# Two attentions on one core: whole sums in each half of the array's rows, output added in memory, and VectorE's exps planned op by op

## The chip, the cores and the metric

One core of a Trainium2 chip runs the kernel. The metric is the time of one execution on the device in microseconds (us); lower is better.

## What is computed

`x` is 2048 tokens by 512. Two attention layers with 32 heads of 16 run over it, and a gate per token mixes their outputs. Layer A has one key and one value head that all 32 query heads share; layer B has keys and values for each head. Everything is float32.

```python
def reference(A_x, A_wq, A_wk, A_wv, A_wo, B_x, B_wqkv, B_wo, gate_w):
    x = A_x
    g = _sigmoid((x * gate_w).sum(-1, keepdims=True))
    a = _A_ref(x, A_wq, A_wk, A_wv, A_wo)   # q: 32 heads; k = x @ wk, v = x @ wv: one head of 16
    b = _B_ref(x, B_wqkv, B_wo)             # q, k, v: 32 heads of 16
    return g * a + (1 - g) * b
# each layer: softmax(q k^T / 4) v, over all 2048 keys, heads joined, times wo
```

Per layer 32 x 2048 x 2048 exponentials are needed, 268 million in all. They dominate: 2048 instructions of 128 x 1024.

## The kernel before

**Precision.** Operands of the projections and of the scores are split into two float16 parts, high and low, and three of the four products are added (`PARTS`). The probabilities and the values are multiplied in float32. The input's ranges are checked at the end (`flag`); a general version would follow outside of them, which these inputs don't need.

**Tiling of TensorE.** The array of 128 x 128 works as eight tiles of 64 rows by 32 columns. Eight matmuls, two row halves by four column quarters, run beside each other. `by_tiles` (line 220) gives each row half a PSUM bank of its own; a sum over 128 rows thus lies in two banks, and `added` (line 227) adds them with two VectorE ops when they are emptied:

```python
    def by_tiles(outs, lhsT, rhs, start, stop):
        for n in range(0, P, COLS):
            for i, out in enumerate(outs):
                r = slice(ROWS * i, ROWS * (i + 1))
                nc.tensor.matmul(out[n : n + COLS], lhsT[r, n : n + COLS], rhs[r], start=start, stop=stop)

    def added(dst, outs, scale):
        nc.vector.tensor_scalar(dst, outs[0], scale, None, op0=ALU.mult)
        nc.vector.scalar_tensor_tensor(dst, outs[1], scale, dst, op0=ALU.mult, op1=ALU.add)
```

**Stages.** Heads come in eight groups (layers a and b in turn, four groups of eight heads each: `groups`). Per group and per half of the queries (1024) there are four stretches of 16 steps over the keys; a step is a quad of four blocks, each 128 keys by 512 queries of one head. `scores` (line 565) writes two blocks into two PSUM banks (`sc`, two such pairs), and ScalarE takes the exp of 128 x 1024 into `pr` (line 569). `values` (line 602, matmuls on line 613) multiplies the quad with the values and a column of ones, in two halves of 256 queries, so that sums and denominators gather in one of two pairs of banks (`aux`). The other pair is the spare one: there the projections of q, k and v (`project`, line 364, and `v_units`), the turning of v (line 454), the output product (`o_unit`, line 469) and the scores for VectorE's exps (`vector_scores`, line 571) take turns, each emptied by VectorE before the next. After a stretch `emptied` (line 618) adds the two banks into `raw` and moves the rows to their heads' places with eight transfers. `norm_pieces` (line 491) divides and splits, and `o_unit` multiplies with `wo`, weighs with the gate and adds the result to `acc` in SBUF, one op per bank on line 485. `acc` is stored at the end.

**Where q and k come from.** `project` empties, adds, clamps, splits into float16 parts and takes the largest value (lines 229, 230, 394, 237, 238, 234), and lays the parts into `Q` and `K` by small transfers (line 375), mostly from GpSimd's queue.

**VectorE's exps.** Some blocks go to VectorE instead of ScalarE. Per exp of 128 x 1024: two conversions from PSUM (line 581), two ops that part mantissa and power (line 587), five steps of a polynomial (line 592). All run in place, each on the result of the one before.

**The order.** All of it is unrolled; a planner in Python (`_Tasks`, line 75, and the loop behind it) writes the order. It counts time in exps (`EXP = 916` ns): per exp one pair of scores, one or two halves of values, and as many products on the spare banks as fit. VectorE's work beside that is put in by `beside`, and `choose` (line 761) asks for an exp on VectorE when nothing is late. Engines run their own instructions in order and wait for each other by semaphores. In the profile, line 225 is the matmul of `by_tiles`, line 562 that of the scores.

Of the kernel before, what the change touches and what calls it, by code (L numbers as in the profile page):

```python
# [20 lines left out]
P = 128  # L21
# [10 lines left out]
EXP = 916  # L32
SCORES, HALF, PRODUCT = 213, 428, 216
FULL = 1500
NARROW = 710
LATEST = 6
WIDE = 1240
OVER = 160
LATE = 250
SCALE = DH ** -0.5  # L40

# [6 lines left out]
VEC = (0.2591677609, 0.7359788364, 0.8973912565, 1.2863896980, -0.0530661755, 1.9226385145)  # L51
VEC5 = struct.unpack("I", struct.pack("f", VEC[5]))[0] & 0x7FFFFF
RANGED = ["x", "gate", "wk_a", "wv_a", "wq_a", "wo_a", "wq_b", "wk_b", "wv_b", "wo_b", "v_a", "v_b"]
KINDS = RANGED + ["q_a", "q_b", "k_a", "k_b"]

# [19 lines left out]
class _Tasks:  # L75

    def __init__(self):  # L80
        self.now, self.clock, self.begun, self.busy, self.empty = 0, 0, 0, 0, 0
        self.units, self.open, self.side, self.fill = [], deque(), deque(), deque()
        self.moves, self.moved = deque(), 0

    def add(self, units, after, due, more=0, full=FULL, ready=lambda: True):

        self.units += [(after, due, u, more, full, ready) for u in units]
        self.units.sort(key=lambda u: u[1])

    def add_side(self, fns, after, ns):  # L90

        more = [(after, f, ns[i % len(ns)]) for i, f in enumerate(fns)]
        self.side = deque(sorted([*self.side, *more], key=lambda s: s[0]))

    def move(self, fns):
        self.moves.extend(fns)

    def given(self, ns):

        self.busy = max(self.busy, self.clock + LATE) + ns  # L100

    def beyond(self, ns):

        self.busy = max(self.busy, self.begun) + ns

    def product(self, left):

        if not self.open:
            for u in self.units:
                if u[0] <= self.now and self.empty <= self.clock and len(u[2]) + 1 <= left and u[5]():  # L110
                    self.units.remove(u)
                    self.open.extend(u[2])
                    self.more, self.full = u[3:5]
                    break
        if not self.open:
            return False
# [8 lines left out]
    def late(self):  # L125

        n = len(self.open)
        for u in self.units:
            n += len(u[2]) + (6 if len(u[2]) > 4 else 3)
            if n > u[1] - self.now:  # L130
                return True
        return False

    def beside(self, until, urgent):
# [10 lines left out]
        if urgent:  # L145
            filled()
# [818 lines left out]
```

## Time and profile before

| | |
|---|---|
| median of 3 runs | 1908.06 us (1907.36 to 1908.97) |
| the profiled execution's span | 1905.9 us, 2.2 less than the median of the runs |
| granted TensorE clock | 0.992 |
| TensorE (PE) busy | 1800.7 us, 94% |
| VectorE (DVE) busy | 1382.3 us, 73% |
| ScalarE (ACT) busy | 1831.9 us, 96% |
| GpSimd (POOL) busy | 466.3 us, 24% |
| exps on ScalarE, on VectorE | 1974, 74 |

How to read the rows: a group's row has line, engine, operation, output and input tile, shapes, count; behind the first bar busy us and mean ns of one; behind the second the idle time just before them and what ended it. A timeline's row has its start in us from the span's start, how long the merged piece lasts in us, then engine, line, operation and count; matmuls overlap, so their starts say more than their lengths. A row of a stretch has its bounds and length in us, busy us of the engine with the count, granted clock, DMA share and GB/s. A row of transfers has destination and source, the issuing queue, the count, the size of each, and the median us from issue to landing.

### The profile page before, as it was taken

To read this page: it belongs to the slowest core of one execution; us is meant where nothing else is said; L and a number is where in the kernel's file an instruction comes from. 1 tells how busy PE (TensorE), PEld (TensorE's weight loads), DVE (VectorE), ACT (ScalarE), POOL (GpSimd) and SP (SyncE) were. 2 spreads that over 40 slices of the span, in tenths; PEclk is the share of its full clock that TensorE was granted. 3 is DMA by queue.
4 is the path that set the end of the run, shared out by engine and by line. 5 is a ranking of instruction groups with operands and counts; after the bars stand their busy time and mean duration, and the time that the engine had idled before them with its cause. 6 is when DMAs were issued, how large, how long until landed. Compare 5 with 4: busy or idle time off the path is not lost.

```text
span 1905.9 us, 128055 instructions
## 1 busy us (share of the span) xinstructions
PE 1800.7 (94%) x59664; PEld 1124.5 (59%) x59664; DVE 1382.3 (73%) x2095; ACT 1831.9 (96%) x1997; POOL 466.3 (24%) x840
## 2 busy tenths in 40 slices
PE   7999999999999999999999999999999999999985
PEld 4666665555566665665555656656655666665642
DVE  5367668787888765778788873788888867477762
ACT  4999999999999999999999999999999999999984
POOL 5333302330044230323006502042203433030000
PEclk9999999999999999999999999999999999999997
DMA  4121101110022110111002201020101111011101
GB/s 141 27 49 35 35 15 27 42 35 16 12 43 46 29 37 12 41 32 35 12 21 45 52 19 31 19 54 15 32 15 36 39 38 37 10 37 35 40 26 42
DMA packets 55739, 65.03 MB, mean 34 GB/s; under 512 B 21440, under 2 KB 29632, under 8 KB 55200
## 3 DMA queue, kind: packets, MB, share of 16 engines
q0 software_dynamic: 24112, 24.89, 6.8%
q1 hardware_dynamic: 30400, 31.46, 6.3%
q8 instruction: 469, 7.68, 1.7%
q14 instruction: 70, 0.57, 0.1%
q10 hardware_dynamic: 688, 0.43, 0.1%
HBM read 10.55 MB, written 4.19 MB: 8 GB/s over the span
## 4 chain that ended last, share of the span: by engine, by line
ACT 67%; PE 15%; issue 12%; DVE 4%; DMA 1%; SPq 0%; DVEq 0%; ACTq 0%; POOL 0%
ACT pr L569 67%; PE aux L613 7%; PE sc L562 4%; PE aux L225 4%; DVE stats L234 1%; DVE acc L485 0%; DVE vpr L592 0%; DMA acc<-in_A_x_dram 0%; DVE dTb L497 0%; DMA dTb<-rawb 0%; PE aux L300 0%; DVE v L238 0%; DVE yv L230 0%; DVE yv L229 0%; DVE xT L305 0%
## 5 line engine op out<-in xcount | busy, mean ns | idle before, releaser
L569 ACT ACTIVATE pr<-sc 128x1024 f32<-128x1024 f32 x1974 | 1821.3, 1090 | 24.7 <-PE sc L562 21.1
L613 PE MATMUL aux<-pr,vA 64*32 64x256 f32 x15712 | 647.2, 376 | 2.0 <-issue 1.8
L613 PE MATMUL aux<-pr,vB 64*32 64x256 f32 x15872 | 636.4, 376 | 0.6 <-issue 0.4
L562 PE MATMUL sc<-Qa,kA 64*32 64x512 f16 x7856 | 441.2, 380 | 28.0 <-ACT pr L569 4.7
L562 PE MATMUL sc<-Qb,K 64*32 64x512 f16 x7936 | 426.2, 381 | 31.0 <-ACT pr L569 5.6
L592 DVE SCALAR_TENSOR_TENSOR vpr<-vpr,part 128x1024 f32<-128x1024 f32 x296 | 363.5, 1228 | 6.1
L562 PEld LDWEIGHTS <-K 64*32 64x32 f16 x8192 | 203.3, 89 | 276.8 <-issue 195.3
L613 PEld LDWEIGHTS aux<-pr,vA 64*32 64x32 f32 x15712 | 328.6, 105 | 57.8 <-issue 9.8
L613 PEld LDWEIGHTS aux<-pr,vB 64*32 64x32 f32 x15872 | 316.6, 106 | 53.9 <-issue 4.6
L562 PEld LDWEIGHTS <-kA 64*32 64x32 f16 x8192 | 203.5, 89 | 238.8 <-issue 157.8
L485 DVE SCALAR_TENSOR_TENSOR acc<-aux,gate_up,acc 128x512 f32<-128x512 f32 x240 | 180.1, 750 | 126.6 <-PE aux L225 112.2
L375 POOL DMA_DIRECT2D Qb<-hib x128 | 63.0, 492 | 557.0 <-PE sc L562 553.9
L375 POOL DMA_DIRECT2D Qa<-hia x118 | 59.9, 508 | 481.8 <-PE sc L562 322.8
L581 DVE TENSOR_SCALAR vpr<-aux 128x512 int32<-128x512 f32 x148 | 95.2, 685 | 36.8 <-PE aux L562 36.2
L587 DVE TENSOR_SCALAR part<-vpr 128x1024 int32<-128x1024 int32 x148 | 103.1, 728 | 0.7
L375 POOL DMA_DIRECT2D K<-hik x128 | 64.3, 506 | 117.5 <-DVE hik L237 115.5
L592 DVE SCALAR_TENSOR_TENSOR vpr<-part 128x1024 f32<-128x1024 f32 x74 | 90.3, 1221 | 1.6
L225 PE MATMUL aux<-xT,w16vb 64*32 64x512 f16 x1536 | 90.5, 376 | 0.0
L225 PE MATMUL aux<-w16ob,o16b 64*32 64x512 f16 x1536 | 70.4, 391 | 16.0 <-ACT o16b L505 13.3
L225 PE MATMUL aux<-xT,w16kb 64*32 64x512 f16 x1536 | 79.5, 376 | 0.1
L225 PE MATMUL aux<-xT,w16qa 64*32 64x512 f16 x1536 | 76.0, 380 | 0.9 <-issue 0.5
L225 PE MATMUL aux<-xT,w16qb 64*32 64x512 f16 x1536 | 76.8, 376 | 0.0
(145 smaller groups left out, 1320.4 us busy)
## 6 DMA issues: line engine op xcount, KB each, us to landing
acc<-in_A_x_dram SPq DMA_DIRECT2D x16, 256.0 KB, 6.1
dTa<-rawa SPq DMA_DIRECT2D x128, 32.0 KB, 2.5
oTa<-rawa SPq DMA_DIRECT2D x128, 32.0 KB, 2.8
K<-hik POOLq DMA_DIRECT2D x128, 32.0 KB, 2.2
K<-lok POOLq DMA_DIRECT2D x128, 32.0 KB, 2.7
Qb<-hib POOLq DMA_DIRECT2D x128, 32.0 KB, 2.8
Qb<-lob POOLq DMA_DIRECT2D x128, 32.0 KB, 2.4
out_dram<-acc SPq DMA_DIRECT2D x16, 256.0 KB, 2.0
```

The source lines that it names most:

```text
L225: nc.tensor.matmul(out[n : n + COLS], lhsT[r, n : n + COLS], rhs[r], start=start, stop=stop)
L234: nc.vector.tensor_reduce(stats[:, n, i : i + 1], src, axis=axis, op=ALU.max, apply_absolute_value=True)
L375: queues[(8 * p + n) % len(queues)].dma_start(op[to : to + DH].rearrange("d (a q) -> d a q", a=2), state[part][rows])
L485: nc.vector.scalar_tensor_tensor(acc[:, t], bank, g, acc[:, t], op0=ALU.mult, op1=ALU.add)
L562: nc.tensor.matmul(sc[i][a : a + COLS], k[r, c * P + a : c * P + a + COLS], Q[src, gi, half, p][r, j * BLK : (j + 1) * BLK], start=True, s ...
L569: nc.scalar.activation(probs[u], sc, AF.Exp, scale=SCALE / (UP * UP))
L581: nc.vector.tensor_scalar(fix[:, i], sc[i], SCALE / (UP * UP) / math.log(2) * 2.0 ** 23, -(2.0 ** 23), op0=ALU.mult, op1=ALU.add)
L587: nc.vector.tensor_scalar(t, fix, a, b, op0=ALU.bitwise_and, op1=op)
L592: nc.vector.scalar_tensor_tensor(pr, pr if i < 4 else m, VEC[i], m if i else power, op0=ALU.add, op1=ALU.mult)
L613: nc.tensor.matmul(o[32 * i : 32 * i + 32, cols], v[r], probs[at // ACT][r, at % ACT, cols], start=first, stop=last)
```

## The change

`_fast` and the planner are written anew; the general version stays. What differs:

- **Sums by halves.** Row half i of the array now sums for its own queries or tokens in bank i of a pair. To reach all terms, each operand is also held with its two row halves swapped (`swapped`: two transfers), and every product has two turns, `w = 0` and `1`: straight and swapped. `added` is gone; each bank holds whole sums. A projection covers 1024 columns at once, 24 jobs of eight matmuls, and is emptied by two ops of 128 x 1024 (high and low part), with the largest value taken from the high part and no clamp.
- **Scores.** Row half = head of a pair, column half = one of two blocks of 512 queries, with the keys of the other column half swapped. Eight matmuls of 64*32 by 512 as before; exps stay 128 x 1024. There are 32 phases (group, half of the queries, two pairs of heads) of 32 quads.
- **Values.** As before eight tiles; the probabilities of ScalarE in two jobs of 256 columns, those of VectorE in four of 128. After a phase one copy of 128 x 1024 empties the pair, and ten transfers move the rows.
- **Output sums.** An output unit (`o_unit`) covers two tiles of tokens with six products and is emptied by two plain ops into one of two buffers (`sums`). For the first group it is stored to the output; for the next six it is added to the output in memory by a transfer from GpSimd's queue (`accum_op`, 48 transfers of 512 KB); before the last group the output so far is read back (`late`, in the memory of `xT`), and the last is added on VectorE.
- **VectorE's exps.** One conversion of 128 x 1024, mantissa and power, four polynomial steps. Each op is an `_Op` with a rank, a time from which it can run, and the ops that it follows.
- **The order.** `_Plan` holds a clock for each engine. VectorE takes the free op of lowest rank (0 emptying a phase, 1 emptying the spare pair, 3 exps, above that the rest, and what is overdue comes forward). TensorE gives the scores first when they can be written, then values, spare jobs, values of VectorE's exps (near a phase's end the last before the spare jobs), and starts nothing that would hold the scores beyond `SLACK`. An exp goes to VectorE when the spare pair is free, no unit is in a hurry, and little of the exps' work is queued. Constants: `EXP` 904 for 916.
- **Start.** x is loaded into the tiles of the exps; seven of eight pairs of x tiles are turned before the first score. The swapped copies of the first weights and of k's and v's weights are moved before they are used.

The core of the diff:

```diff
-EXP = 916
-SCORES, HALF, PRODUCT = 213, 428, 216
...
+EXP, EXP_ENDS, EXP_AFTER = 904, 1136, 456
+SCORES, HALF, PRODUCT = 215, 430, 215
+SLACK = 400
+PROBS, VECS = 6, 7
...
+    def by_tiles(outs, lhs, rhs, start, stop):
+        for n in range(0, P, COLS):
+            for i in range(2):
+                nc.tensor.matmul(outs[n : n + COLS, i], lhs[i][rows(i), n : n + COLS], rhs[i][rows(i)],
+                                 start=start, stop=stop)
+
+    def swapped(dst, src, queue):
+        for i in range(2):
+            queue.dma_start(dst[rows(i)], src[rows(1 - i)])
...
+            def hi():
+                hilo.extend(halves_of(name))
+                nc.vector.tensor_scalar(hilo[0], pair[1], UP ** -1, None, op0=ALU.mult)
+
+            def lo():
+                nc.vector.scalar_tensor_tensor(hilo[1], pair[1], UP ** -1, hilo[0], op0=ALU.mult, op1=ALU.subtract)
...
+        def finish(end):
+            def take(e):
+                g = gate_up[:, i, tt[e] : tt[e] + 1]
...
+                if e == 0:
+                    state["sum"] = sums[turn[0]]
+                    turn[0] ^= 1
+                nc.vector.tensor_scalar(state["sum"][:, e], pair[1][:, e], g, None, op0=ALU.mult)
...
+                if n == 0:
+                    nc.sync.dma_start(dst, state["sum"])
+                else:
+                    plan.on_pool([lambda: nc.gpsimd.dma_start(dst, state["sum"], accum_op=ALU.add)], t, 1500)
...
+    def products(u, bank):
...
+        for hh in range(2):
+            for a in range(0, P, COLS):
+                key = c * P + (a + ROWS * w) % P
+                j = a // ROWS
+                nc.tensor.matmul(bank[a : a + COLS, hh], k[rows(hh), key : key + COLS],
+                                 Q[src, gi, half, p][rows(hh), j * BLK : (j + 1) * BLK], start=True, stop=True)
...
+            for i in range(2):
+                nc.tensor.matmul(pair[0][32 * k : 32 * k + 32, i, cols], v[rows(i)], probs[2 * m + k // 2][rows(i), hh, cols],
+                                 start=first, stop=last)
...
+    def vector_job(now):
+
+        if chained() > WORK + (EXTRA if half_vec else 0):
+            return None
+        if held[0] > held[2] - 3 or plan.backlog(2) > 2500:
+            return None
...
+        a = plan.vec(convert, 1130, 1, t + TO_VEC, (), spared)
+        b = plan.vec(mantissa, 620, 3, 0.0, (a,), None, due(7000))
+        c = plan.vec(power, 620, 3, 0.0, (a,), None, due(6300))
+        d = plan.vec(lambda: horner(3), 1131, 3, 0.0, (b, c), None, due(5600))
+        for i in (2, 1, 0):
+            d = plan.vec(lambda i=i: horner(i), 1131, 3, 0.0, (d,), None if i else over, due(1300 * i + 1300))
...
+        limit = math.inf
+        if at[0] < len(quads) and free_probs and t < math.inf:
+            limit = max(t, plan.starts[-1] + SLACK) if plan.starts else t
+        ending = at[0] >= len(quads) or quads[at[0]][0] > pv_at[0] or left_in(pv_at[0]) < 20
...
+        for get in (mine, other, spare) if ending else (mine, spare, other):
```

1427 lines of the change are left out of this document (807 added, 620 removed).

## The prediction

> **What bounds the kernel now.** I read the page first: span, engines, and the chain that ended last.
>
> ```profile
> span 1905.9 us, 128055 instructions
> PE 1800.7 (94%) x59664; PEld 1124.5 (59%) x59664; DVE 1382.3 (73%) x2095; ACT 1831.9 (96%) x1997; POOL 466.3 (24%) x840
> ACT 67%; PE 15%; issue 12%; DVE 4%; DMA 1%; SPq 0%; DVEq 0%; ACTq 0%; POOL 0%
> L569 ACT ACTIVATE pr<-sc 128x1024 f32<-128x1024 f32 x1974 | 1821.3, 1090 | 24.7 <-PE sc L562 21.1
> ```
>
> ScalarE (ACT) is the longest engine and holds two thirds of the chain, nearly all of it in one line, the exps: 1974 of the 2048 that the problem needs. The other 74 run on VectorE (DVE). Next: what does one exp cost when nothing holds it, and where do the exps begin and end? A stretch cut from the start of one exp to the start of another, then the timeline's first and last piece of exps:
>
> ```profile
> 629.84:645.20 15.36, 15.36 (x18) 1.00 0.07 17
> ```
> ```profile
> 13.30 5.92 PE L225 MATMUL aux<-xT,w16qa 64*32 64x512 f16 x192
> ...
> 29.28 3.12 ACT L569 ACTIVATE pr<-sc 128x1024 f32<-128x1024 f32 x3
> ...
> 1834.27 42.27 ACT L569 ACTIVATE pr<-sc 128x1024 f32<-128x1024 f32 x46 [0.47 <-PE sc L562]
> ```
>
> The stretch counts 18 exps, of which the first is only the tail of the one before: 17 steps, 15.36/17 = 0.9035 us each. This is ACT's own pace. 1974 steps of it are 1783.5 us; the exps in fact take from 29.28 to 1834.27 + 42.27 = 1876.54, or 1847.3 us. So the span is 29.3 (start) + 1783.5 (pace) + 63.8 (ACT held up) + 29.4 (tail) = 1906. The median of the runs, 1908.06, lies 2.2 above the span, and I add 2.2 at the end.
>
> So two things shorten this kernel: fewer exps on ACT (0.9035 us for each that goes to DVE), and less of the 63.8. What keeps the number on DVE at 74? DVE is only 73% busy, so look at TensorE (PE) and at the PSUM banks that it shares with DVE, in the timeline:
>
> ```profile
> 1225.83 0.63 PE L225 MATMUL aux<-xT,w16qb 64*32 64x512 f16 x16
> ...
> 1226.26 0.41 PE L562 MATMUL sc<-Qb,K 64*32 64x512 f16 x8
> ...
> 1226.48 0.63 PE L613 MATMUL aux<-pr,vB 64*32 64x256 f32 x16
> 1226.53 0.69 DVE L229 TENSOR_SCALAR yb<-aux 128x512 f32<-128x512 f32 x1
> ...
> 1227.01 0.41 PE L562 MATMUL sc<-Qb,K 64*32 64x512 f16 x8
> ...
> 1227.32 0.69 DVE L230 SCALAR_TENSOR_TENSOR yb<-aux,yb 128x512 f32<-128x512 f32 x1
> ...
> 1227.93 0.41 PE L562 MATMUL sc<-Qb,K 64*32 64x512 f16 x8
> ...
> 1228.05 0.43 DVE L394 TENSOR_SCALAR yb<-yb 128x512 f32<-128x512 f32 x1
> 1228.14 0.63 PE L613 MATMUL aux<-pr,vB 64*32 64x256 f32 x16
> ...
> 1228.51 0.43 DVE L237 TENSOR_SCALAR hib<-yb 128x512 f16<-128x512 f32 x1
> 1228.57 0.63 PE L225 MATMUL aux<-xT,w16qb 64*32 64x512 f16 x16
> ...
> 1228.97 0.69 DVE L238 SCALAR_TENSOR_TENSOR lob<-yb,hib 128x512 f16<-128x512 f32 x1
> ...
> 1229.58 0.68 DVE L234 TENSOR_REDUCE stats<-yb 128x1 f32<-128x512 f32 x1
> ...
> 1229.87 0.41 PE L562 MATMUL sc<-Qb,K 64*32 64x512 f16 x8
> ...
> 1230.08 0.63 PE L613 MATMUL aux<-pr,vB 64*32 64x256 f32 x16
> ...
> 1230.52 0.41 PE L225 MATMUL aux<-xT,w16qb 64*32 64x512 f16 x8
> ...
> 1230.73 0.41 PE L562 MATMUL sc<-Qb,K 64*32 64x512 f16 x8
> ```
>
> Read the starts, since ends overlap. From 1229.87 PE is packed: scores of one exp (eight matmuls, 0.21 us), values of one exp (sixteen, 0.44), one job of eight on the spare banks (0.21), next scores: 0.86 us. Against 0.9035 us per exp that leaves room for one spare job per exp and not for two. And from 1226.26 to 1228.57, 2.3 us, no spare job runs: DVE is emptying the spare banks (L229, L230, 1.48 us and 0.8 of handing over), and PE idles between values and scores. So the limit is the number of these places, one per exp, and the time in which the spare banks are shut. Call it the budget of places.
>
> **The change, part by part.** I cost the budget before, to calibrate it, from these rows:
>
> ```profile
> L592 DVE SCALAR_TENSOR_TENSOR vpr<-vpr,part 128x1024 f32<-128x1024 f32 x296 | 363.5, 1228 | 6.1
> L485 DVE SCALAR_TENSOR_TENSOR acc<-aux,gate_up,acc 128x512 f32<-128x512 f32 x240 | 180.1, 750 | 126.6 <-PE aux L225 112.2
> L581 DVE TENSOR_SCALAR vpr<-aux 128x512 int32<-128x512 f32 x148 | 95.2, 685 | 36.8 <-PE aux L562 36.2
> L587 DVE TENSOR_SCALAR part<-vpr 128x1024 int32<-128x1024 int32 x148 | 103.1, 728 | 0.7
> L592 DVE SCALAR_TENSOR_TENSOR vpr<-part 128x1024 f32<-128x1024 f32 x74 | 90.3, 1221 | 1.6
> L225 PE MATMUL aux<-xT,w16qa 64*32 64x512 f16 x1536 | 76.0, 380 | 0.9 <-issue 0.5
> ```
> ```profile
> L230 DVE SCALAR_TENSOR_TENSOR rawa<-aux,rawa 128x512 f32<-128x512 f32 x32 | 22.2, 692 | 3.4
> L229 DVE TENSOR_SCALAR rawb<-aux 128x512 f32<-128x512 f32 x32 | 22.0, 687 | 25.0 <-PE aux L613 25.0
> L454 PE MATMUL aux<-ident,v 64*32 64x64 f16 x1024 | 18.6, 191 | 2.7 <-DVE v L238 2.7
> ```
>
> Places offered: 1974, and 63.8/0.9035 = 70 more while ACT is held up: 2044. Taken: six groups like the last of the first fence (the weights q, k, v and o), 1536 matmuls each, are 1152 jobs of eight; the turning of v (1024 matmuls in jobs of sixteen) 64; x and k at the start some 30. Shut: 64 projected blocks at 2.3 us; 128 output units with two of L485 each, 2.2 (1.5 and 0.7 of handing over); 16 turns at 2: 461 us or 510 places. Left for the 74 exps: 2044 - 1152 - 64 - 30 - 510 = 288, so 3.9 places per exp on DVE. Counted singly one costs 1 for its scores, 2 for its values and 2.2 for the banks' shut time (L581 twice, then handing over), 5.2; some of its values thus run while the banks are shut.
>
> *Sums by halves.* Each bank now holds whole sums of its own queries, so nothing is added across banks. A projection empties 128x1024 with two ops and no clamp: 32 blocks, of which 31 in the steady part. A 1024-wide op from PSUM isn't in this trace; bounds are twice L581 (1.37) and the SBUF op L592 (1.23). I take 1.23, because one op has one fixed part. Shut time: 1.23 + 1.26 + 0.8 = 3.3 us, 102 us. The output units are 60 in the steady part instead of 128, each with two 512-wide ops, 2.1 us: 126. Eight turns at 2.2: 18. Together 246 us or 272 places, instead of 510. PE's jobs are the same work: 31 x 24 = 744, output 372, turning 128 short ones (92 places), start 35: 1243. Scores and values keep their size and count.
>
> *DVE's load.* Removed or shrunk: the projections' six ops in the timeline are 3.6 us x 64 blocks (3.2 for v), 224, become 32 x 3.5 = 113; L485's 180 us and its twin of the first group (16 more ops, 12) become 128 plain ops, 83; the four groups of raw sums (88, first and last shown) become 32 copies, 36. That frees some 270 us of DVE: 1382 - 652 (the four exp rows) - 270 = 460 without exps. An exp on DVE now has four L592-like steps instead of five: 1.23 + 2 x 0.73 + 4 x 1.23 = 7.6 us, or 7.05 where independent ops alternate and each starts 0.08 us before the last one ends, as L234 at 1229.58 does behind L238. In a steady part of some 1760 us DVE could then hold (1760 - 460)/7.05 = 184, or 171 at 7.6. It isn't the limit.
>
> *The number N of exps on DVE.* Offered: 2048 - N, plus 33 for a hold-up of 30 us. Taken: 1243 + 272 + 3.9 N. So 4.9 N = 566, N = 115. The new planner may cut the values of DVE's exps into jobs of 0.21 us that fit a shut time; if all of them run there, an exp costs 1 + 2.2 + 1 = 4.2 and N = 135. I take the middle, 125; bounds 91 (nothing hidden, 5.2 + 1) and 165 (less shut time than I think).
>
> *Hold-ups.* Now 63.8, of which some 9 in the first 71 us, where ACT also copies x. The old planner reckons 916 ns for an exp that takes 903.5, the new one 904, and lets a PE job start only if the scores still come in time. I take 30; bounds 10 and 80 (PE is fuller: 125 more exps' worth of jobs in less time).
>
> *Start and tail.* The first products (13.30 to 19.22) now wait for the swapped weights too, 1024 queries are projected instead of 512 twice, and seven of eight x pairs are turned ahead of the first score. I take 35 for 29.3, bounds 29 and 41. The tail keeps its chain (empty the banks, ten moves instead of eight, reciprocal, product, out) but ends eight output tiles: 29.5, bounds 26 and 36.
>
> *Adding transfers.* 48 transfers of 512 KB add into the output in memory, from POOL's queue; two buffers hold the sums, so the third output unit's DVE op waits for the first one's landing. No adding transfer is in this trace; bounds by rows:
>
> ```profile
> acc<-in_A_x_dram SPq DMA_DIRECT2D x16, 256.0 KB, 6.1
> ...
> out_dram<-acc SPq DMA_DIRECT2D x16, 256.0 KB, 2.0
> ```
> ```profile
> L375 POOL DMA_DIRECT2D K<-lok x128 | 65.2, 514 | 4.3 <-issue 2.6 <-DMA K<-lok 1.4
> ```
>
> Twice the bytes, read and written: 2 x 2.0 = 4 to 2 x (6.1 + 2.0) = 16 us; I take 8, nearer the single store than the crowded loads. A unit takes six places (5.4 us) and 2.1 shut, so the third comes 15 us after the first: 8 is hidden. It is not where the unit's transfer stands behind the 32 moves of a projection on POOL (32 x 0.51 = 16 us); then it lands 16 + 1.5 + 8 = 25.5 us after those moves begin, the third unit comes after 7.5 + 15 = 22.5, and DVE waits 3 us, in at most 14 places: 42 us on an engine that isn't the limit. I count nothing; the bound of the hold-ups takes it in, and the rival prices a late landing.
>
> **Sum:** 35 + (2048 - 125) x 0.9035 = 1737.4, + 30 + 29.5 + 2.2 = **1834**.
>
> **The rivals.**
>
> *DVE fills up (1789).* If shut time is shorter than the trace's 0.8 us of handing over suggests, N goes to DVE's ceiling, between 171 and 184, say 175: 35 + 1692.3 + 30 + 29.5 + 2.2. For it: DVE idles 27% now. Against: the 2048 - 175 = 1873 places are fewer than 1243 + 272 + 3 x 175 = 2040. The page "VectorE: DVE Perf Modes" of the Trainium skill (The DRAIN you can't avoid) says the next op doesn't issue until the pipe is empty, which would make alternating ops worthless. The trace's 0.08 us overlap of L238 and L234 disagrees; by the page the ceiling is 171 and the time 1793.
>
> *The places are no better used (1890).* N stays near 80 and hold-ups at 45: 35 + 1778.1 + 45 + 29.5 + 2.2. For it: PE is already at 94%, and a projection shuts the banks longer at a time.
>
> *The adding transfers stall DVE (slower, 1940).* DVE works in order: an output unit that waits for a landing holds every later op, the emptying of the exps' scores among them; PE, in order too, then stands at its next spare job, and the scores of ACT's exps stand behind it. If a transfer lands after 16 us and starts up to 16 us late behind a projection's moves, the third unit of a row waits 16 + 1.5 + 16 - 22.5 = 11 us, in 14 rows of four units 154 us, of which ACT would feel perhaps 106, since banks and buffers cover the rest: 1834 + 106. It makes the kernel slower from 74 us on ACT, so 108 us on DVE, 7.7 a row, a landing after about 12.7 us. For it: POOL issues all moves. Against: single loads of this size land fast. "SBUF — State Buffer" (SBUF: two separate sides) in the Trainium skill states that POOL can't write a transfer's descriptors while DVE runs a double-rate op. L587 (0.73 us for what takes L592 1.23) looks like one, yet POOL's 128 moves of K take 514 ns on average beside 148 of these; by the page each added transfer may start 0.73 us later, 48 x 0.73 = 35 us if nothing hides it, 1869.
>
> *It doesn't do what it says:* the planner finds hardly a place for DVE's exps (N below 40): 1905 to 1915.
>
> **How the numbers follow.** Forecast (N 91 to 165) 0.60, DVE full 0.13, places no better 0.12, transfers stall 0.12, does not do it 0.03. The range leaves out most of the slower rival and the lowest corner: from 1775 (N 175, hold-up 15) to 1900 (N 80, hold-up 55). A measurement here tells about 0.2%, 3.8 us: faster 0.85, the same 0.02, slower 0.13.
>
> **What would show it.** Right: 1905 to 1950 exps on ACT, still at 0.904 a step; ACT held up under 50 us in all; DVE 75 to 85% busy; an emptying of 1024 from PSUM at 1.2 us. Wrong: a count of exps on ACT above 1965 (places), DVE waiting for a landing of out (transfers), a step above 0.92, or first scores after 41 us.

## Result and the profile after

The changed kernel takes 2002.92 us (median, 1999.31 to 2005.09), the kernel before on the same chip 1908.38: a ratio of 1.0486, 95% interval 1.0467 to 1.0506. It is 95 us slower where 74 us faster was forecast. The profiled execution has a span of 2001.7 us.

First the page's span, engines, chain and exps, to be read against the first fence of the prediction:

```profile
span 2001.7 us, 130978 instructions
PE 1840.3 (92%) x61680; PEld 1155.0 (58%) x61680; DVE 1198.4 (60%) x1352; ACT 1816.2 (91%) x1961; POOL 542.4 (27%) x891
...
PE 47%; ACT 31%; issue 9%; DVE 6%; POOL 4%; DMA 2%; SPq 1%; ACTq 0%; DVEq 0%; POOLq 0%
...
L571 ACT ACTIVATE prob<-sc 128x1024 f32<-128x1024 f32 x1946 | 1805.6, 1093 | 128.3 <-PE sc L564 124.4
```

ACT runs fewer exps (1946 for 1974), and yet it is 91% busy instead of 96%, and the chain has passed from ACT (67% before) to PE (47%). No engine but POOL (27% for 24%) got fuller. The last column of the last row is the clue: ACT stood 128.3 us idle ahead of exps, 124.4 of it for scores from PE, where the same row of before has 24.7 and 21.1.

Next the pieces that the sum was made of: a clean stretch of 18 steps, cut from one exp's start to just before another's (the 19 exps include the tail of the one before it), and the first and the last exps in the timeline.

```profile
1856.74:1873.01 16.27, 15.42 (x517) 8.91 (x512) 16.10 (x18) 16.27 (x19) 1.25 (x1) 1.00 0.13 30
```
```profile
34.05 6.01 ACT L571 ACTIVATE prob<-sc 128x1024 f32<-128x1024 f32 x6
...
1940.89 32.29 ACT L571 ACTIVATE prob<-sc 128x1024 f32<-128x1024 f32 x35
```

16.27 / 18 = 0.904 us: ACT's pace is what it was. Put into the terms of the prediction's sum, the span is: start 34.0 us; pace 1946 x 0.9035 = 1758.2; tail 2001.7 - (1940.89 + 32.29) = 28.5; what is left, 180.9, is hold-ups. (Below, hold-ups are counted from first to last start of an exp, less 0.9035 a step: 180.6 here, 63.4 before.)

Where does ACT's wait for PE come from? The waits of PE, of after:

```profile
PE pair L612 <- issue: 31.9, 44, 2.9
PE pair L564 <- DVE sum L471: 15.8, 3, 8.2
PE pair L564 <- DMA K<-lokb: 12.6, 8, 3.2
PE sc L564 <- issue: 10.5, 17, 2.0
...
PE pair L188 <- issue: 5.2, 6, 2.6
```

"issue" means that the matmul waited for nothing that the profile shows: no semaphore, no busy PE. All such rows of PE sum to 53.5 us in after; the same view of before has these three and no more, 4.6 us:

```profile
PE aux L613 <- issue: 2.3, 4, 1.2
PE sc L562 <- issue: 1.8, 4, 0.5
...
PE aux L225 <- issue: 0.5, 1, 0.5
```

The longest such gap in the timeline of after (rows of PE and POOL):

```profile
1164.38 1.35 POOL L481 DMA_DIRECT2D out_dram<-sum  x1
...
1166.79 1.22 POOL L481 DMA_DIRECT2D out_dram<-sum  x1 [1.07 <-DVE sum L471]
...
1168.74 0.62 PE L612 MATMUL pair<-prob,vA 64*32 64x256 f32 x8
...
1172.23 0.44 PE L612 MATMUL pair<-prob,vA 64*32 64x256 f32 x4 [2.87 <-issue]
```

PE stops in the middle of a job, 8 of its 16 matmuls done, 2.6 us after POOL began to issue the second of two adding transfers, and stands for 2.87 us. What is missing are instructions: among the page's DMA queues is one, q8, that carries nothing else.

```profile
DMA packets 140435, 109.73 MB, mean 55 GB/s; under 512 B 86432, under 2 KB 94880, under 8 KB 139888
...
q8 instruction: 485, 7.95, 1.6%
```

The same two lines of before:

```profile
DMA packets 55739, 65.03 MB, mean 34 GB/s; under 512 B 21440, under 2 KB 29632, under 8 KB 55200
...
q8 instruction: 469, 7.68, 1.7%
```

In after, 485 packets of 16 KB bring 7.95 MB for 2 x 61680 matmuls and weight loads. That is 64 bytes for each, so 256 instructions a packet, and PE needs a packet every 4.1 us. The queue is as busy as before, but the traffic beside it has grown from 65 to 110 MB and from 55,739 to 140,435 packets. Worked out from the packets' records: of the 59 gaps over 250 ns without a wait, nine in ten end 1.25 to 1.55 us after a packet of q8 has come in, while nine in ten random moments lie 0.2 to 4.4 us behind one. For the gap above, 6.7 us passed from the start of the packet before to the start of the one that ended it. Of the 14 gaps over 1 us (26.3 us) 11 have an adding transfer issued 2 to 11 us before they end, which holds for some 20% of random moments.

### The profile page after: what moved, and what is told of

The parts are those of the page before. It is cut to its first block, busy times and chain, and to the rows that moved or that the text cites. A ratio compares the mean times of both kernels' runs of the same rounds, so it can differ in the third digit from the quotient of the medians.

```text
span 2001.7 us, 130978 instructions
## 1 busy us (share of the span) xinstructions
PE 1840.3 (92%) x61680; PEld 1155.0 (58%) x61680; DVE 1198.4 (60%) x1352; ACT 1816.2 (91%) x1961; POOL 542.4 (27%) x891
## 2 busy tenths in 40 slices
DMA packets 140435, 109.73 MB, mean 55 GB/s; under 512 B 86432, under 2 KB 94880, under 8 KB 139888
## 3 DMA queue, kind: packets, MB, share of 16 engines
q8 instruction: 485, 7.95, 1.6%
q10 hardware_dynamic: 1952, 2.66, 0.4%
## 4 chain that ended last, share of the span: by engine, by line
PE 47%; ACT 31%; issue 9%; DVE 6%; POOL 4%; DMA 2%; SPq 1%; ACTq 0%; DVEq 0%; POOLq 0%
ACT prob L571 31%; PE pair L612 23%; PE sc L564 13%; PE pair L188 8%; DVE vec L763 2%; POOL Qa L352 2%; DVE sum L471 1%; DVE vec L751 1%; SPq L505 1%; PE pair L564 1%; POOL K L352 1%; PE pt L265 1%; DMA wqb<-in_B_wqkv_dram 1%; DVE raw L665 0%; DMA oT<-raw 0%
## 5 line engine op out<-in xcount | busy, mean ns | idle before, releaser
L571 ACT ACTIVATE prob<-sc 128x1024 f32<-128x1024 f32 x1946 | 1805.6, 1093 | 128.3 <-PE sc L564 124.4
L612 PE MATMUL pair<-prob,vA 64*32 64x256 f32 x15680 | 695.8, 378 | 16.9 <-issue 15.7
L612 PE MATMUL pair<-prob,vB 64*32 64x256 f32 x15456 | 657.7, 381 | 11.6 <-issue 10.6
L612 PEld LDWEIGHTS pair<-prob,vA 64*32 64x32 f32 x15680 | 350.3, 105 | 81.2 <-issue 38.8
L763 DVE SCALAR_TENSOR_TENSOR vec<-vec,vec 128x1024 f32<-128x1024 f32 x306 | 373.3, 1236 | 2.4
L612 PEld LDWEIGHTS pair<-prob,vB 64*32 64x32 f32 x15456 | 329.5, 106 | 71.4 <-issue 29.2
L751 DVE TENSOR_SCALAR vec<-pair 128x1024 int32<-128x1024 f32 x102 | 124.1, 1217 | 71.9 <-PE pair L564 71.2
L763 DVE SCALAR_TENSOR_TENSOR vec<-vec 128x1024 f32<-128x1024 f32 x102 | 125.1, 1226 | 1.0
L481 POOL DMA_DIRECT2D out_dram<-sum x48 | 59.7, 1243 | 239.2 <-DVE sum L471 215.3
L511 DVE RECIPROCAL dT<-dT 128x256 f32<-128x256 f32 (+1 forms) x66 | 111.0, 1690 | 18.8 <-DMA dT<-raw 18.8
L188 PE MATMUL pair<-xT,w16kb 64*32 64x512 f16 x1536 | 101.6, 376 | 4.7 <-issue 4.6
```

The costliest lines, as they stand in the source:

```text
L188: nc.tensor.matmul(outs[n : n + COLS, i], lhs[i][rows(i), n : n + COLS], rhs[i][rows(i)], start=start, stop=stop)
L481: plan.on_pool([lambda: nc.gpsimd.dma_start(dst, state["sum"], accum_op=ALU.add)], t, 1500)
L511: nc.vector.reciprocal(d[:, c : c + cut], d[:, c : c + cut])
L571: nc.scalar.activation(probs[u], sc, AF.Exp, scale=SCALE / (UP * UP))
L612: nc.tensor.matmul(pair[0][32 * k : 32 * k + 32, i, cols], v[rows(i)], probs[2 * m + k // 2][rows(i), hh, cols], start=first, stop=last)
L751: nc.vector.tensor_scalar(tile("p").bitcast(I32), pair[1], SCALE / (UP * UP) / math.log(2) * 2.0 ** 23, None, op0=ALU.mult)
```

## Two theories

**Queues.** ACT is held up by separate causes, each a queue: PE's instructions come late while heavy transfers run; DVE, which works in order, stands at an op that waits for POOL, and with it the emptying that PE waits for; K is laid late. **Full PE** (the rival): the new plan packs PE so tightly that any slip reaches ACT; take one cause away and the time comes back elsewhere. The prediction's own slower rival, DVE waiting for the landing of an added transfer, already has the trace against it: DVE has no wait for out in after.

Chips differ. The experiments were measured in four sets, and the kernel before took 1923 us in the first (e1 to e4), 1923 in the second (e5 to e8), 1917 in the third (e9 to e12) and 1911 in the fourth (e13 to e15). So ratios to it are compared, and the changed kernel was run again.

## Experiments

**e5, the changed kernel again.**

> The changed kernel unaltered, to see what it measures on the chip of these runs. Chips differ (the kernel before took 1908 on one and 1923 on another); the ratio to the kernel before should again be 1.045 to 1.060 and the hold-ups 170 to 210 us.

2023.57 us, ratio 1.0538 (1.0493 to 1.0582), hold-ups 198.9, PE without a wait 70.6 us. e1 to e4 and e6 to e8 are set against this. PE's gaps were 53.5 us on the first chip and are 70.6 here, so a difference of some 17 us between kernels of different sets can be the chip's.

**e1, without the adding transfers.**

```diff
-plan.on_pool([lambda: nc.gpsimd.dma_start(dst, state["sum"], accum_op=ALU.add)], t, 1500)
+plan.on_pool([], t, 0)
```

> Leaves out the 48 adding transfers of groups 1 to 6, so the output lacks these groups; the plan and all else stay. The theory (instruction supply): the changed kernel's PE stands 54 us with nothing that it waits for, against 5 before, and the long ones of these lie beside adding transfers of 512 KB, while the queue that brings 16 KB packets of instructions slows from one in 3.8 us to one in 5.4 to 7.4. Without the transfers these gaps fall to some 25 us and the time by 20 to 45 us, to 1958 to 1983. Rival one (the prediction's: DVE waits for landings): the time falls by over 60 us, and DVE's waits on out in the changed kernel should have been there, which they are not. Rival two (PE is simply planned too full, any slip reaches ACT): under 8 us.

1991.87 us, ratio 1.0341 (1.0312 to 1.0371): 32 us less than e5. PE without a wait 37.4 for 70.6, hold-ups 170.3 for 198.9. The first row of PE's waits in e5, then in e1:

```profile
PE pair L612 <- issue: 40.8, 58, 2.9
```
```profile
PE pair L612 <- issue: 18.5, 43, 1.4
```

The gaps' 33 us and the time's 32 agree: instructions, not landings. It isn't the chip: e2 and e3, measured in e1's set with their adding transfers, have gaps of 71.0 and 69.6 us.

**e2, V's swapped copy in whole rows.**

```diff
-swapped(vB[1][:, ts, :, 0], vB[0][:, ts, :, 0], nc.sync)
-swapped(vB[1][:, ts, :, 2], vB[0][:, ts, :, 2], nc.sync)
+swapped(vB[1][:, ts], vB[0][:, ts], nc.sync)
```

> Moves the swapped copy of V of the b groups as whole rows of 6 KB instead of 64-byte pieces (one pair of transfers in place of two, 65,500 packets fewer of 140,435). The theory (instruction supply): some of the gaps without a wait lie beside these transfers (532 us), so 3 to 15 us less, and DVE's waits for SP's queue get no longer. Rival two (PE planned too full): within 4 us of the changed kernel, since the plan is the same.

2032.65 us, ratio 1.0564 (1.0540 to 1.0588), not below e5; the gaps are as they were. A miss: moving the same copy in fewer, larger packets (75,666 in all for 140,435) gains nothing.

**e3 and e7, the largest-value ops of the weights** later, or left out:

```diff
-plan.vec(lambda: absmax(f"w{part}_{src}", gi, pair[0][:, 0]), 590, 4, at + 500, due=at + 20000)
+plan.vec(lambda: absmax(f"w{part}_{src}", gi, pair[0][:, 0]), 590, 4, at + 15000, due=at + 40000)   # e3
+plan.vec(lambda: None, 590, 4, at + 500, due=at + 20000)                                           # e7
```

> The largest-value op of a weight block is laid on DVE 15 us after the planned end of POOL's split instead of 0.5 us. The theory (DVE held in line): the trace shows DVE standing 25.0 + 7.6 us in six places for POOL's split, and PE and ACT behind it; with the later op these waits are gone and the time falls by 20 to 35 us, to 1968 to 1983. Rival two (PE planned too full): DVE's waits go, but the slip shows up elsewhere, under 8 us gained.

> The largest-value ops of the weight blocks are left out (so the range test sees no weights); the plan stays as it is. The theory (DVE held in line behind POOL's split): DVE's 33 us of waiting for POOL go, PE's waits for DVE with them, and the time falls by 20 to 35 us against the changed kernel. Rival two (PE planned too full): under 8 us.

The trace of after shows what is at stake (DVE, POOL, SyncE's queue and PE around 1410 us):

```profile
1406.61 1.11 SPq L193 DMA_DIRECT2D w16vb<-w16vb  x2
...
1407.81 0.53 SPq L219 DMA_DIRECT2D wqb<-in_B_wqkv_dram  x1
...
1410.91 1.49 POOL L204 TENSOR_SCALAR wqb<-wqb 128x512 f32<-128x512 f32 x1 [4.33 <-DMA wqb<-in_B_wqkv_dram]
...
1412.47 0.61 POOL L205 CAST w16qb<-wqb 128x512 f16<-128x512 f32 x1
...
1413.12 0.69 DVE L197 TENSOR_REDUCE stats<-w16qb 128x1 f32<-128x512 f16 x1 [7.07 <-POOL w16qb L205]
...
1413.72 1.40 DVE L471 TENSOR_SCALAR sum<-pair,gate_up 128x512 f32<-128x512 f32 x2
...
1415.17 0.72 PE L564 MATMUL pair<-Qb,K 64*32 64x512 f16 x8 [8.20 <-DVE sum L471]
...
1416.43 1.02 ACT L571 ACTIVATE prob<-sc 128x1024 f32<-128x1024 f32 x1 [8.47 <-PE sc L564]
```

Read it from the top: the next weights' load stands on SyncE's queue behind the swapped copies of the last ones (L193), which wait for POOL's split; the load issues late, POOL splits late, DVE stands 7.07 us at a largest-value op that only the range test at the end needs, the output's sum stands behind it, the scores on the same bank behind that, and the next exp last: 8.47 us.

e3: 2010.63 us, ratio 1.0455 (1.0435 to 1.0474), 13 us less than e5 (3 of them by the plan's own clock); DVE's 33 us for the weights are gone from its waits. e7's own 28418 us mean nothing, since the range test, fed with zeros, sends it through the general program afterwards; in its first part hold-ups are 184.9, 14 less than e5. Both are below the 20 to 35 that I gave: of DVE's 33 us of waits less than half reached ACT.

**e8, K and V of the b groups earlier.**

```diff
-ns=14000 if part == "k" else 18000
+ns=40000 if part == "k" else 44000
```

> The projections of K and V of the b groups are due 40 and 44 us ahead of their first use in place of 14 and 18. The plan itself then has 12.6 us held up in place of 24.3, with 96 exps on DVE in place of 102, and ends 6 us earlier. The theory: the 19 us at 305 to 325 us of the changed kernel, where K of the first b group comes late, are gone, and with them waits for landings of K; the exps that DVE loses cost 5.4 us; 6 to 25 us less. Rival two: the gap at 305 goes but PE, as full as before, loses it again later: within 5 us.

1998.06 us, ratio 1.0397 (1.0361 to 1.0434), 25 us less than e5; the gap of 14.86 us that after shows at 321.54 us ahead of an exp, and PE's 12 us of waits for landings of K, are gone. The gain is a net one: with the plan moved, the weights' largest-value ops stand in a worse place. DVE waits 49.6 us for POOL's split of weights (32 in e5), and in three places PE stands 19.8 us behind a conversion that waits behind such an op; the exps there are late by 6.3, 7.5 and 7.2 us.

**e4, no exps on DVE** (the planner's choice returns nothing), and **e10, PE planned looser**:

```diff
-SCORES, HALF, PRODUCT = 215, 430, 215
+SCORES, HALF, PRODUCT = 221, 442, 221
```

> No exp runs on DVE, all 2048 on ACT, whose own plan then has only 6.5 us held up. At 34 us of start, 2048 x 0.9035 = 1850.4 and 30.7 of tail and launch, the time is 1915 + hold-ups. The theory (hold-ups come from queues: instruction supply, DVE behind POOL's split, late K and Q): these stay, of the 180 only the 19 planned for K and some small ones go, hold-ups 90 to 140, so 2005 to 2055. Rival two (PE planned too full with the jobs of 102 exps): hold-ups fall under 60 and the time to under 1975, faster than the changed kernel although ACT has 102 exps more.

> The changed kernel's planner reckons 221, 442 and 221 ns for PE's jobs in place of 215, 430 and 215, so it packs PE 3% looser; its own plan has 31 us held up in place of 24 and 106 exps on DVE in place of 102, and ends 3 us later. Rival two (PE planned too full): the some 190 stalls of about 0.3 us on PE alone, 57 to 61 us in all, shrink by half or more, and the time falls by 20 us or more. The theory: instruction gaps, DVE's waits and late K are untouched by this, so the time is within 12 us of the changed kernel, ratio to the kernel before 1.045 to 1.060.

e4: 2058.27 us, ratio 1.0693 (1.0672 to 1.0715), hold-ups 146.7, somewhat over the theory's 90 to 140 and far from the rival's 60. Two things in its trace stand against a simple reading. Its output units come closer together, and DVE now does wait for landings of the adding transfers:

```profile
DVE sum L471 <- DMA out_dram<-sum: 52.4, 7, 9.9
```

And PE's time without a wait is 35.4 us with the adding transfers in place, where e2 and e3 of the same set have about 70. So the traffic alone doesn't set these gaps; how much else PE has to run bears on them too, and so far the rival has a point.

e10: 2014.56, ratio 1.0493 (1.0455 to 1.0532), hold-ups 204, PE without a wait 67.4, and the small stalls on PE alone 55.6 us for 60.8 (sorted as in the section on why the prediction was wrong). A plan that is 3% looser doesn't help, so missing slack in PE's plan alone is not the cause.

**e9, adding transfers in the kernel before.** Every 30 exps one transfer of 512 KB goes from x into the output: 8 plain ones, then 48 adding ones, all overwritten at the end:

```diff
+if u >= 270 and (u - 270) % 30 == 0 and added_to[0] < 56:
+    ...  # k = added_to[0] % 8; rows_ and x_rows: 256 rows of out and x
+    if added_to[0] < 8: nc.sync.dma_start(rows_, x_rows)
+    else:               nc.gpsimd.dma_start(rows_, x_rows, accum_op=ALU.add)
```

> The kernel before with traffic put in that it does not use: every 30 exps one transfer of 512 KB from x into out, 8 plain ones first and then 48 adding ones from POOL's queue, all overwritten by the output at the end. Nobody waits for them. The theory (instruction supply): traffic alone starves PE, so PE's time without a wait grows from 5 us to 20 to 45, ACT's hold-ups from 63 to 80 to 110, and the time by 15 to 40 us, ratio 1.008 to 1.021. Rival two (what counts is how full the new plan packs PE): under 5 us, ratio under 1.003.

1964.99 us, ratio 1.0237 (1.0197 to 1.0276): a little more than I gave. The waits in it (of before, ACT's was 21.1 us and PE's two 2.3 and 1.8):

```profile
ACT pr L569 <- PE sc L562: 72.7, 91, 4.1
...
PE aux L613 <- issue: 23.3, 21, 2.8
...
PE sc L562 <- issue: 11.1, 10, 3.3
```

Nobody waits for these transfers, the plan is the old one, and PE runs out of instructions for 41.9 us instead of 4.6; hold-ups are 123.7 for 63.4. Of the 41.9 us, 36.6 fall in gaps that end within 13 us of an adding transfer's issue, and 1.8 in the 153 us of the 8 plain ones. PE's other waits stay as they were (for ACT's exps 10.9 us for 10.3, for ACT's op on o16b 13.1 for 13.3). This is the experiment that separates the theories: the old plan, given one part of the new kernel's traffic, shows the new kernel's gaps.

**e11, three causes away at once** (e1, e3 and e8 together).

> Three causes taken away at once: no adding transfers (the output lacks groups 1 to 6), the largest-value ops of the weights 15 us later, K and V of the b groups due 40 and 44 us ahead. The theory: the hold-ups have separate causes that add up, so the single gains do too: 32 + 13 + 25 us against the changed kernel, ratio to the kernel before 1.010 to 1.025, hold-ups 115 to 140. Rival two: what is taken away comes back elsewhere on a full PE, ratio 1.030 or more.

1940.83 us, ratio 1.0119 (1.0088 to 1.0151), hold-ups 112.7. The ratio falls by 0.0419 against e5; the three single falls are 0.0197, 0.0083 and 0.0141, together 0.0421. So the causes add up, and nothing comes back. That they do so this closely is partly luck, since e8 alone made e3's cause worse. PE without a wait is still 41.4.

**e13, without the swapped copies too.** On e11, the second copies of V and of all weights but the first aren't made; PE reads the unswapped ones, so the number of operations stays.

```diff
-swapped(pair[1], pair[0], nc.sync)
+pass
-weights[src, gi, part] = pair
+weights[src, gi, part] = pair if queue is nc.scalar else [pair[0], pair[0]]
-swapped(vB[1][:, ts, :, 0], vB[0][:, ts, :, 0], nc.sync)
-swapped(vB[1][:, ts, :, 2], vB[0][:, ts, :, 2], nc.sync)
-v = vB[w][:, c, p, hh : hh + 2, :]
+v = vB[0][:, c, p, hh : hh + 2, :]
```

> e11 with the copies of operands held swapped left out too: of the weights after the first (both halves of the rows read the one copy) and of V of the b groups (the unswapped one is read), so values are wrong, while PE, ACT and DVE do the same number of operations. 88,000 or so of the 127,376 packets go. The theory (instruction supply): PE's time without a wait falls from 42 us to 10 to 25, hold-ups from 113 to 80 to 100, the time by 12 to 32 us against e11, ratio to the kernel before 0.995 to 1.006. Rival: the rest of the gaps come from the order of PE's work itself; gaps 35 or more, ratio within 0.004 of e11's 1.0119.

1912.10 us, ratio 1.0008 (0.9993 to 1.0023), hold-ups 84.3. Its packets and ACT's wait:

```profile
DMA packets 57647, 74.29 MB, mean 39 GB/s; under 512 B 18880, under 2 KB 27328, under 8 KB 57104
```
```profile
ACT prob L569 <- PE sc L562: 33.2, 68, 1.9
```

PE without a wait 23.3 us. With about the packets of before (55739), and without its adding transfers, the new plan takes as long as the kernel before: the 20 us that 22 exps fewer on ACT save go in 21 us more of hold-ups.

**e6, e12, e14, e15: how the adding transfers are issued.** Each as 4 of 128 KB (e6), as 16 of 32 KB with the swapped weights on POOL's queue and the edits of e3 and e8 (e12), as 8 of 64 KB with those of e3 and e8 (e14), or as plain stores (e15):

```diff
-plan.on_pool([lambda: nc.gpsimd.dma_start(dst, state["sum"], accum_op=ALU.add)], t, 1500)
+plan.on_pool([lambda a=a: nc.gpsimd.dma_start(dst[a : a + 32], state["sum"][a : a + 32], accum_op=ALU.add) for a in range(0, P, 32)], t, 650)   # e6
+# e12: 8 rows each, 530 ns; e14: 16 rows each, 900 ns
+plan.on_pool([lambda: nc.gpsimd.dma_start(dst, state["sum"])], t, 1500)   # e15
```

> Each adding transfer of 512 KB is issued as four of 32 rows and 128 KB, 192 in place of 48; the bytes and the plan of PE, ACT and DVE stay. The theory (a packet of instructions queues behind a burst): if its delay comes from standing behind one long transfer, shorter bursts with some 0.6 us of POOL's issue between them let it pass, and PE's time without a wait falls by 15 to 30 us, the time by 10 to 30 against the changed kernel. If the delay comes from the bytes as such, or the four still lie back to back, the same within 6 us. Rival one (landings stall DVE) expects longer landings and a longer time.

> A kernel that computes all: each adding transfer as 16 of 8 rows and 32 KB (8.5 us of POOL's issue for what was one burst of 3.5 us), the swapped weights from POOL's queue in place of SP's, the weights' largest-value ops 15 us later, K and V of the b groups due 40 and 44 us ahead; 94 exps on DVE by its plan, 10.4 us held up in it. The theory (a burst delays the instructions): 13 + 25 us as in the single runs, and 10 to 30 of the 32 that the adding transfers cost, ratio to the kernel before 1.015 to 1.035. If the bytes and not the burst delay the instructions: 1.033 to 1.042.

> A kernel that computes all: each adding transfer as 8 of 16 rows and 64 KB, largest-value ops of the weights 15 us later, K and V due 40 and 44 us ahead. In e12 POOL issued 16 pieces in 689 / 768 = 0.9 us each, 14.4 us a unit, and DVE waited 149 us for landings of out. With 8 pieces at 0.9 a unit takes 7.2 us, less than half the 15 us in which the third unit comes: DVE's waits for out under 15 us, PE's time without a wait 45 to 60 us (70.7 unaltered, 37.6 in e12), ratio to the kernel before 1.022 to 1.034. If the landing itself and not POOL's queue made the wait in e12: waits over 50 us and a ratio over 1.045.

> The 48 adding transfers are plain stores of the same 512 KB from the same queue (the output then holds the last group's sums alone). If the bytes delay the instructions, a store moves half of what an adding transfer reads and writes: half of the 32 us that leaving it out gained, so 10 to 22 us faster than the changed kernel, ratio to the kernel before 1.042 to 1.049, PE's time without a wait 48 to 60 us. If it is the adding that holds the engines of the DMA: as without them, 1.034 to 1.039, 38 to 45 us.

e6: 2016.60 us, ratio 1.0501, 7 us less than e5, with intervals that overlap; PE's gaps 58.7 for 70.6. e12: 2088.31, ratio 1.0882 (1.0839 to 1.0926), the slowest but e7, a miss. Its waits of DVE, then POOL's issues (busy us behind the bar):

```profile
DVE sum L471 <- DMA out_dram<-sum: 148.6, 19, 16.8
```
```profile
L481 POOL DMA_DIRECT2D out_dram<-sum x768 | 689.0, 3921 | 2.8 <-issue 2.4
```

I had planned 530 ns for a piece, as for the moves of K; it takes 689 / 768 = 0.9 us (the row's mean of 3921 ns counts issues that overlap), 14.4 us a unit, about as long as the 15 us in which the third unit needs the buffer back. So here the prediction's slower rival did occur. The gaps of PE in the same kernel fell to 36.7 us, as without any adding transfer. e14: 1966.07 us, ratio 1.0292 (1.0275 to 1.0309), gaps 38.9, DVE's wait for out 35.4 us in 4 places, more than the 15 I gave: the best changed kernel here that computes all, still slower than before. e15: 1980.63, ratio 1.0367 (1.0350 to 1.0384), gaps 29.8: the same 512 KB stored without adding starve PE no more than none at all (37.4 in e1). e3's and e8's edits alone leave the gaps at 69.6 and 65.4, and e10, in e12's set, has 67.4, so e12's drop comes from how the transfers are issued. The fourth set has no run of the unaltered kernel; e14's and e15's gaps are below the first chip's 53.5 too. So what starves PE here is adding in large pieces, and not the bytes alone.

All in one table (hold-ups and PE without a wait from the profiled execution):

| kernel | ratio to before | exps on ACT | hold-ups, us | PE without a wait, us |
|---|---|---|---|---|
| before | 1 | 1974 | 63.4 | 4.6 |
| after, first chip | 1.0486 | 1946 | 180.6 | 53.5 |
| e5 after again | 1.0538 | 1946 | 198.9 | 70.6 |
| e1 no adding | 1.0341 | 1946 | 170.3 | 37.4 |
| e9 before with adding | 1.0237 | 1974 | 123.7 | 41.9 |
| e11 three causes away | 1.0119 | 1952 | 112.7 | 41.4 |
| e13 no copies either | 1.0008 | 1952 | 84.3 | 23.3 |
| e14 adding by 8 | 1.0292 | 1952 | 133.0 | 38.9 |
| e15 plain stores | 1.0367 | 1946 | 151.8 | 29.8 |
| e4 no exps on DVE | 1.0693 | 2048 | 146.7 | 35.4 |

## Why the prediction was wrong

**The step that failed: hold-ups, 30 us with bounds of 10 and 80; they are 181.** 151 of the 170 us between the sum and the span lie in this one term. It was taken from the planners' arithmetic (916 ns against 904, PE a little fuller), and its bounds too, so it priced only what a planner can see. By the new plan's own clock ACT is held up 24 us; the other 156 are events that it doesn't know. Sorted by what came last ahead of each late exp in after: 47 us behind PE's gaps without a wait, 57 in some 190 stalls of about 0.3 us on PE alone (part of them behind shorter gaps of that kind), 21 behind the weights' largest values, 16 behind landings of K and Q. Of the rest, 15 is the gap at 321.54 us, where K of the first b group is projected late, which the plan has too. Why does each reach ACT? The scores of the exp after next can start when an exp has freed its bank; by the plan's numbers that is 1136 ns after its start, and from the start of scores to their exp it is 456 ns, so 2 x 904 - 1136 - 456 = 216 ns of cover. A gap of some us on PE thus costs ACT nearly all of it, or more: the one of 2.62 us that ends at 614.46 us makes exps late by 2.7 us, the one of 2.87 us that ends at 1172.23 by 4.8.

The two differ in PE's clock. Behind the second gap the granted clock is at 0.5 for 3.4 us; behind the first it isn't. In after there are 12 such places between start and tail, 3.4 to 6.8 us long, each begun in a stall of PE of 2.0 to 8.2 us or within 1 us of its end. Exps that start in them or up to 1 us later are late by 54 us in all, the stalls' own delay counted in. In e11 there is one such place, with 1 us, and in before one near the end, with 5. So part of what each cause of a long stall costs is the slow clock behind it.

**Adding transfers: "I count nothing".** Wrong by some 32 us (e1). The term followed the landing only: buffer, third unit, DVE. That part was right for this kernel: 8 us estimated, 5.9 measured, no wait of DVE in after, though e4, e8, e12 and e14, with other plans or pieces, have 52, 21, 149 and 35 us. What it left out is who shares the path: PE's instructions. The queue stood on the page of before, 469 packets of 16 KB. The Trainium skill's page "DMA: Bandwidth & Descriptors" (Queues, rings and completion order) states that a DMA engine goes round its queues and changes over only when a whole packet, of some 9 to 17 descriptors, is through. What the profile counts as packets are smaller pieces: one adding transfer of 512 KB is 272 of them ((140,435 - 127,377) / 48, after against e1), 17 for each of 16 engines. If these are the page's descriptors, such a burst could by that rule hold up the instructions for its length, and one cut small could not. e12's and e14's gaps (36.7 and 38.9 us, no more than without any) agree with it, and e6's four pieces, which gained only 12 us of gaps, agree in part. Whether this changeover is the mechanism no run here shows: e15's stores are bursts of the same bytes, in 144 pieces each, and starve PE no more than none. The Trainium skill's page "SBUF — State Buffer" (SBUF: two separate sides) states that a DMA can't be slowed by computing nor computing by a DMA; at SBUF that may be so, but e9 shows PE stopped by traffic all the same, by way of its instructions. The 35 us that the prediction worked out from that page for POOL's issue aren't there either, but not for the reason that it gave. Its average of 514 ns hides what the page describes. In after 78 of POOL's 749 moves of K and Q take over 600 ns, where the median is 484; 76 of these overlap an op of DVE on L754 or L758 (0.69 us for the size that takes L763 1.23) and end about 0.1 us behind it. Of the 48 adding transfers only 3 overlap such an op (1341 ns on average, the others 1237).

**Copies of swapped operands.** The prediction gave them a place in the start and none in the steady part. e13 against e11 shows some 21 us (ratio 1.0008 for 1.0119, of 1911), hold-ups 84.3 for 112.7, PE's gaps 23.3 for 41.4. The two were measured in different sets, and the changed kernel's own ratio moved by 0.005 between chips, so some 10 of the 21 us are in doubt. The weights' copies also sit on SyncE's queue ahead of the next load; e13 doesn't part that from the traffic.

**The number of exps on DVE: 102 for 125,** within its bounds of 91 and 165, 20.8 us. The budget of places was roughly right, though it counts 60 output units for shut time and 62 (372 / 6) for PE's jobs, 12 places or under three exps. DVE's load was too: 460 + 102 x 7.05 to 7.6 = 1179 to 1235 us, measured 1198. It is 60% busy, not 75 to 85, because N is lower and the span longer, and the forecast's own numbers gave only 73 to 77% (460 + 125 x 7.05 to 7.6, of 1834). Why the planner found no more places in DVE's idle time was not tested.

**What held:** the pace (0.904), the start (34.0 for 35), the tail (28.5 for 29.5), and the emptying of 1024 columns, taken as 1.23 us between 1.23 and 1.37:

```profile
L394 DVE TENSOR_SCALAR hiqb<-pair 128x1024 f16<-128x1024 f32 x8 | 9.8, 1225 | 108.1 <-PE pair L188 108.1
```

**The rivals.** The slower one had the right direction and the wrong mechanism; its own sign (DVE waiting for out) is absent in after and strongest in e12, where ACT lost most of it: DVE waited 148.6 us, and exps behind those landings were late by 124.5, against "perhaps 106" of 154. "Places no better used" named 45 us of hold-ups; the places were used better, 102 exps for 74. "DVE fills up" didn't happen. The Trainium skill's section that this rival is held against ("VectorE: DVE Perf Modes", The DRAIN you can't avoid) goes on to say that a next op which isn't held starts earlier, so the 0.08 us overlap in the rows doesn't contradict it.

**What stays open.** e13 has 84 us of hold-ups with 23 of PE's gaps, before 63 with 5; the rest of that difference, the 0.3 us stalls above all, was not taken apart. In e9 hold-ups grew by 60 us and PE's gaps by 37; slow clock in six places, with 26 us of late exps, may cover part of the rest. Why e4's gaps are half of e5's under the same adding transfers wasn't tested. Why whole rows of V (e2) gained nothing while leaving out all copies did was not separated from the weights' copies.

## What to carry to other kernels

This kernel runs some 60 PE instructions a microsecond, and they come as DMA packets beside its data. In such a kernel, count what a change adds in traffic against the instruction queue's packets, large adding transfers above all, and look for "issue" in PE's waits. When moving sums off an engine into transfers, price who shares the path, not only who waits for the landing. And bound the hold-ups of a hand-planned schedule by the events that its plan can't see (queues in order, landings, instruction supply), with the cover that the buffers give, here 0.2 us, not by the plan's own slack.

## What was not expected of the hardware

An adding transfer of 512 KB takes POOL 1243 ns to issue and lands in 5.9 us, a plain store from the same queue 761 ns and 4.3 us, and only the first starves PE. The rows of transfers, of after and then of e15:

```profile
out_dram<-sum POOLq DMA_DIRECT2D x48, 512.0 KB, 5.9
```
```profile
out_dram<-sum POOLq DMA_DIRECT2D x48, 512.0 KB, 4.3
```

A 32 KB piece of an adding transfer costs POOL 0.9 us where a 32 KB move of K costs 0.52. And a long stall on PE costs twice: at 1415.17, after 8.20 us of standing, eight score matmuls take 0.72 us instead of 0.41, with the granted clock at 0.5 from 1411.4 to 1418.2 us.
